# Pooled keys loaded on 128 partitions, and the steps of five blocks in one list

## The chip, the cores and the metric

The kernel runs on one NeuronCore of a Trainium2 chip. The metric is the device time of one execution in microseconds, as the median of several runs. A profile of one execution shows what each engine did: TensorE (PE) multiplies matrices into PSUM and loads weights (PEld), VectorE (DVE) and ScalarE (ACT) work on PSUM and SBUF, GpSimd (POOL) works on SBUF and issues the input loads, SyncE (SP) issues the stores and the transposes that a DMA makes.

## The reference

```python
# attention with keys and values averaged over groups of 8 positions
B, H, S, D = 8, 8, 576, 64;  Sp = S // 8          # 72 pooled positions
k_p = k.reshape(B, H, Sp, 8, D).mean(axis=3)
v_p = v.reshape(B, H, Sp, 8, D).mean(axis=3)
scores = q @ k_p.transpose(0, 1, 3, 2) / sqrt(D)
attn = softmax(scores)                            # over the 72 pooled positions
x = (attn @ v_p).transpose(0, 2, 1, 3).reshape(B * S, H * D)      # 4608 x 512
# feed-forward: the largest of three linear maps, then a fourth
h = maximum(maximum(x @ w1, x @ w2), x @ w3)      # w1, w2, w3: 512 x 768
out = h @ w_out                                   # 768 x 512, result 4608 x 512, float32
```

## The kernel before

The eight batches go through attention one by one, and their 576 tokens each fill a ring `xT` of 2048 columns (features on partitions, tokens along the free dimension). The feed-forward reads that ring in nine blocks of 512 tokens, numbered 0 to 8. Attention of batch n+1 is interleaved with the feed-forward of block n, so that PE always has matmuls to do while other engines finish exponentials, evictions and loads. Each engine executes its own instructions strictly in the order in which the program issues them; the order in the code is the order on the engine. Nothing reorders them: the order was written out by hand as lists of short names, and a small interpreter (`middle` for blocks 1 to 5, `weave` for the rest) turns each name into instructions.

What the names stand for, for a batch b (written `b:` where it isn't the block's own) or a block n:

- `k`: keys of the batch. `k-` turns the pooled keys `kp` with matmuls into PSUM (`keys`, `pkt`), `k+` copies them into the two padded tiles `kz` (`turn_k`, L213; DVE writes the first tile, ACT the second, for batches above 2).
- `T`: a DMA transpose, issued by SP, of the batch's queries `qb` into `qT` (L349). `q0` to `q3` do the same on PE, for batch 2.
- `s0`, `s3`, `s6` (and `s70` to `s78` for batch 7): scores on PE (L226), and with `+` their exponentials on ACT (L231) into `et`.
- `v0` to `v4`: the attention output of one 128-token chunk on PE (`values`, L302), with `+` its normalization on DVE (L310, L312) into `xn`.
- `x0` to `x4`: `xn` transposed into the ring `xT`; from batch 3 on by a DMA transpose from SP (L287).
- `h`: one piece of the hidden layer of a block: four matmuls of 512 columns (L419) and, with `+`, an ACT or DVE operation on the result (L425, L427).
- digits `1` to `7`: the seven products of a Strassen-like form of the output matmul (`out_seven`, L765), ten matmuls each, with their evictions to `osb` (L776, L779); `a1` to `a4` and `b1` to `b4` are the DVE sums these products need (`sums_of`, L664). In `weave`, `o1` to `o7` are the same for blocks 5 and 7, `1a` to `7c` are the seven products of the hidden layer (`seven`, L842), `T` there folds x for them, and `F` is one step of a plain projection (`project`, L467, L471).
- `f` and `S`: sums of weights on DVE that the seven-product forms need.
- `k5<`, `v5<`, `q5<`: the load of keys, values or queries of a batch, issued by POOL. Such a load waits for the last hidden matmul issued before it and for the latest query transpose `T`, and everything behind it on POOL waits with it.
- `k5+2`, `v5+2`: the next two operations of the pooling fold on POOL. `!` makes the next such operation wait for the last DVE sum (`gate`).

A name with `-` starts a step (its matmuls), the same name with `+` later ends it (the eviction); a name with neither does both.

POOL computes the pooled keys and values. A load brings keys of one batch as float16 into a tile [96, 6, 8, 64]: 96 partitions, six groups of eight positions each. `fold_steps` (L163 to L167) adds the eight rows of a group in three stages, 4+4 into `half`, 2+2, 1+1, for keys and values alike, the first stage in two operations for batches 3 to 7. Three PE transposes of [96, 128] then turn `kp`. Queries and keys use two buffers each, and so do `qT`, `kz`, `kp` and the tiles of values.

The list of before had one entry per block, 1 to 5; all hidden pieces, products and attention steps of a block's entry came before those of the next.

Of the kernel before, what the change touches and what calls it, by code (L numbers as in the profile page):

```python
# [10 lines left out]
ALU = mybir.AluOpType  # L11
# [3 lines left out]
def kernel(  # L15
# [11 lines left out]
    nc = tc.nc  # L27
# [4 lines left out]
    POOL = 8  # L32
# [40 lines left out]
    def load_k(b, eng, dtype=F16, parts=1):  # L73
# [5 lines left out]
        return [eng.dma_start(out=kts[b][:, i:i + n], in_=src[:, i:i + n])  # L79
                for i in range(0, 6, n)][-1]  # L80

    def load_v(b, eng, dtype=F16, cuts=(0, H)):
        if b == 0:
            vts[0] = ld.tile([96, 4096], dtype, name="vt0", tag="vt")[:, 0:3072].rearrange(
                "p (h i d) -> p h i d", h=H, i=6)
            src = v[0].rearrange("h (p i) d -> p h i d", i=6)
            return [eng.dma_start(out=vts[0][:, h:g], in_=src[:, h:g])
                    for h, g in zip(cuts, cuts[1:])][-1]
        vts[b] = ld.tile([Sp, H, POOL, D], dtype, name="vt", tag="vt")
        src = v[b].rearrange("h (sp j) d -> sp h j d", j=POOL)  # L90
        return [eng.dma_start(out=vts[b][:, h:g], in_=src[:, h:g])
                for h, g in zip(cuts, cuts[1:])][-1]
# [24 lines left out]
    make_identity(nc, ident)  # L117
    identh = const.tile([128, 128], F16, name="identh", tag="identh")
    make_identity(nc, identh)
    load_v(0, nc.gpsimd, cuts=(0, 4, 8))  # L120
    pick = const.tile([96, 6, 128], F16, name="pick", tag="pick")
    nc.gpsimd.memset(pick, 1.0)
# [9 lines left out]
    load_q(1)  # L132
    load_v(1, nc.gpsimd)
    load_q(2)
    load_k(2, nc.gpsimd)
    load_v(2, nc.gpsimd)


# [18 lines left out]
    def fold_steps(e, t, out, dtype=F32, parts=1):  # L157
        part, n = t.shape[:2]
        f = const.tile([part, n, 4, D], dtype, name="half" if dtype == F32 else "halfh",
                       tag="half" if dtype == F32 else "k16")  # L160
        for i in range(0, n, n // parts):
            at = slice(i, i + n // parts)
            yield e.tensor_tensor(out=f[:, at], in0=t[:, at, 0:4, :], in1=t[:, at, 4:8, :],  # L163
                                  op=ALU.add)
        yield e.tensor_tensor(out=f[:, :, 0:2, :], in0=f[:, :, 0:2, :],  # L165
                              in1=f[:, :, 2:4, :], op=ALU.add)
        yield e.tensor_tensor(out=out, in0=f[:, :, 0, :], in1=f[:, :, 1, :], op=ALU.add)  # L167

    def new_kp(b):
        kps[b] = sb2.tile([96, 6, D], BF16, name="kp", tag="kp")  # L170
# [34 lines left out]
        return pkt  # L205

    def turn_k(b):
        pkt = keys(b, ATT if len(pools) < 3 else SC)

        def put():  # L210
            for par, evac in enumerate((nc.vector.tensor_copy, nc.scalar.copy)):
                for odd in range(2):
                    (evac if b > 2 else nc.vector.tensor_copy)(  # L213
                        out=kz_all[b % 2][par][64 * par:64 * par + 64, :, 0:Sp].rearrange(
                             "p h (r i t) -> p h r i t", i=3, t=2)[:, :, :, :, odd],
                        in_=pkt[64 * odd:64 * odd + 64].rearrange(
                             "p i (h r) -> p h r i", r=12))

        return put
# [586 lines left out]
    def seven(n):  # L806
# [41 lines left out]
        def evict(i, g, p):  # L848
# [11 lines left out]
            elif i in (5, 7) and (12 - i, g) in done:  # L860
# [6 lines left out]
              15: [(0, "S S")], 17: [(1, "K")], 18: [(0, "S S")], 24: [(1, "q0 k")], 25: [(1, "q1")],  # L867
              26: [(1, "s0 q2")], 28: [(1, "s3 Q3")], 30: [(1, "s6")], 31: [(1, "v0")],
              32: [(1, "v1 x0")], 33: [(1, "X1 v2 v3")]}, (hidden, project))
    load_k(3, nc.gpsimd)  # L870
    load_v(3, nc.gpsimd)
    load_q(3)
    fold_k(2, nc.gpsimd)
    fold_v(2)


    folding = {}

    def pool_step(n, name):

        what, b = name[0], int(name[1])
        if name[2:] == "<":
            load = {"k": lambda: load_k(b, nc.gpsimd), "v": lambda: load_v(b, nc.gpsimd),
                    "q": lambda: load_q(b)}[what]
            op = load()
            for x in (mms[-1], *turned):
                after([op], x)
            return
        if (what, b) not in folding:
            if what == "k":  # L890
                new_kp(b)
                folding[what, b] = fold_steps(nc.gpsimd, kts[b], kps[b], parts=2)
            else:
                folding[what, b] = fold_steps(nc.gpsimd, vts[b], vp_all[:, b, :, 0:D],
                                                  parts=2)
# [4 lines left out]
            held.clear()  # L900

    ORDER = """
        b1 o1- 2a- b3 o1+ k7- b2 1a- 1b- v62- 1a+ k7+ 2a+ b4 T o6- s70- o6+ o2- s70+ o2+ 6a-
        s71- o5- 7a- s72- 7a+ vpool s71+ 6a+ 1b+ s72+ v62+ s73- v63- 5a- v63+ s74- 6b- x62
        s73+ s75- s74+ 5a+ v64 s76- s75+ x63 s76+ s77- 4a- s77+ s78- 3a- 4a+ 6b+ s78+ 2c-
        o7- o5+ 2b- o7+ x64 3a+ 1c- 5b- v70- o3- v70+ 1c+ x70 6c- 2b+ 6c+ 5b+ v71- o4- 2c+
        3b- o3+ o4+ 2a- T 7b- v71+ 7b+ x71 5c- 3b+ 2b- 5c+ v72- 4b- 1a 4b+ 3c- 7c- 2a+ 7c+
        v72+ 3c+ F 1b- 4c 1b+ v73 x72 6a- 2b+ 6b- 6a+ F 7a- 5a- F 5a+ 6b+ v74- 3a- v74+ x73
        7a+ 3a+ x74 F 1c- 4a- 1c+ 4a+ 2c- 5b 6c- 7b- 6c+ 7b+ 3b- T F 3b+ 2c+ 5c- 1a- 5c+ 4b
        1a+ F 7c 2a- 3c- 2c- 2a+ 3c+ 4c- 6a 4c+ 1b- H 2b- 5a- h 1b+ 5a+ 6b- 7a 3a 6b+ o1 1c-  # L910
        5b- 4a- 5b+ o2- 1c+ 6c- 4a+ 6c+ 7b- 2b+ 7b+ 3b- o6- 2c+ 5c- o6+ o2+ 4b- 5c+ o5- 4b+
        o5+ 7c o7- 3b+ 3c- 4c- o7+ o3- 4c+ o4- 3c+ o3+ o4+
    """

    def weave():

        products, seen, outs = {}, {}, out_seven(5)
        for name in ORDER.split():
            if name == "F":
                next(tiles)  # L920
            elif name == "vpool":
                held[:] = gate
                pool_step(5, "v7+4")
            elif name[0] == "b":
                sums_of(5, name)
            elif name == "H":
# [19 lines left out]
                else:  # L946
                    parts(name, begin)

    MIDDLE = {
        1: """  # L950
            h- q4< k4< h+ 1:x2 1:v4- h- h- v4< h+ 1:v4+ h+ h- 1:x3 h- h+ h+ h- 1:x4 h+ h- k-
            h- h+ h+ q0 h h- k+ h+ h q1 h s0- s0+ s0+ q2 h- s0+ h- s0+ h+ b1 S q3 h+ h- S S
            3:T S h+ a3 s3- a1 s3+ s3+ h- s3+ h- h+ h+ a2 h- s3+ a4 s6- s6+ 1- s6+ h+ b3 b2
            b4 v0 2- 1+ 6- x0 v1 7- v2- 6+ x1 5- 2+ 7+ v2+ ! k3+4 v3- v3+2 v3+ 5+ v4 3- x2
            4- x3 3+ 4+ x4
        """,
        2: """
            h k5< k- h- k+ h+ a1 a3 h- a2 f a4 f ! v3+2 v5< h+ f s0- s0+ s0+ s0+ h- h- h- h+
            h+ s0+ h- h+ s3- h+ h- f s3+ h- s3+ h+ h- s3+ b1 s3+ s6- h+ s6+ h- h+ h- s6+ !
            k4+2 h+ h+ b2 b3 b4 ! k4+2 1- 4:T v0- 1+ v1- v0+ x0 2- v1+ 6- v2- 7- x1 2+ 7+  # L960
            v4+2 6+ v2+ 5- v3- 5+ v3+ x2 x3 v4 x4 3- 4 3+
        """,
        3: """
            k- q5< k+ a3 k6< h a1 h- h- h+ a2 s0- f a4 ! v4+2 s0+ s0+ f h- h+ s0+ h+ s0+ h-
            h- h+ h+ s3- h- v6< h+ h s3+ s3+ s3+ s3+ h- b1 h- h+ h+ s6- s6+ ! k5+2 h h- s6+
            1- h+ b2 b3 b4 1+ ! k5+2 v5+2 v0- 2- v0+ x0 v1 6- 2+ x1 6+ 7- 5:T 7+ v2- 5- v2+
            x2 v3- 5+ v3+ v4 x3 3 x4 4
        """,
        4: """
            h- q6< h+ k- h- k+ a1 a2 f h+ h- a3 a4 ! v5+2 h- f h+ k7< h+ s0- s0+ h- h- s0+  # L970
            s0+ h+ s0+ h+ 6:T h- s3- h+ s3+ s3+ s3+ h- s3+ h+ h- b1 h+ h ! k6+2 s6- s6+ h h
            b3 b2 b4 s6+ ! k6+2 1- v6+2 v0 2- 1+ x0 v1- 6- v1+ 2+ x1 v2 7- 6+ 5- x2 v3 6:k-
            x3 7+ 5+ 3- 6:k+ v4 x4 4- 3+ 4+
        """,
        5: """
            h q7< a1 v7< h- a2 h- a3 h+ h+ a4 ! v6+2 h- s0- s0+ h+ s0+ h- s0+ s0+ h- h- k7+4
            h+ h+ s3- h+ 7:T s3+ h- s3+ h- s3+ s3+ h+ s6- h+ s6+ s6+ h h- v0 h+ h- x0 v1- h+
            v1+ x1
        """}
    folds = iter([f for wi in range(1, 3) for f in [fold_w(wi)] * 4])  # L980

    def middle(n):

        pieces, outs, out_tiles = hidden(n), None, project(n)
        for name in MIDDLE[n].split():
            if name[0] == "h":
                parts(name, lambda: next(pieces))
            elif name == "F":
                next(out_tiles)
            elif name == "f":  # L990
                next(next(folds))
            elif name == "!":
                held[:] = gate
            elif name[0].isdigit() and name[1:] in ("", "+", "-"):
                outs = outs or out_seven(n)
                parts(f"o{name}", lambda: outs(int(name[0]), 0, 1))
            elif name[0] in "ab":
                sums_of(n, name)
            elif name[2:3] == "<" or name[2:3] == "+" and name[3:]:
                pool_step(n, name)  # L1000
            else:
                b, _, step = name.rpartition(":")
                do(int(b or n + 1), step)
        assert next(pieces, None) is None

    tt_all.append(const.tile([128, 4, 5, HALF], F16, name="tt", tag="tt"))
    for n in range(1, 6):
        middle(n)
    assert next(folds, None) is None
    pad2 = const.tile([128, 3, 2, HALF], F16, name="pad2", tag="k16")  # L1010
    pad3 = ld.tile([128, 8, 2, HALF], F16, name="pad3", tag="vt")
# [47 lines left out]
```

## Time and profile before

| | us |
|---|---|
| median of 3 runs (226.77 to 227.67) | 226.8 |
| the profiled execution | 227.08 |
| its span, from the first to the last instruction | 225.4 |
| PE busy in the span | 212.3 |
| PE's last matmul ends | 221.5 |
| POOL busy in the span | 140.9 |

The TensorE clock was granted in full (1.0) through the whole span. In the 40 slices of the span, POOL's and PE's busy tenths read:

```profile
PE   6688999999999999999999999999799999999993
...
POOL 7974300999939969775885769794292903881020
PEclk9999999999999999999999999999999999999999
DMA  6999999999649999649967999699530755200265
```

PE is near its limit in all slices but the first four, the 29th and the last. The DMA engines are full until about 55 us while the weights and the first three batches arrive.

### The profile page before, as it was taken

The page shows a single profiled execution, that of the slowest core. Times are in us where ns is not written, and L with a number is a line of the kernel's source. Part 1 is how long each engine was busy: PE and PEld are TensorE (multiplying, and loading weights), DVE is VectorE, ACT ScalarE, POOL GpSimd, SP SyncE. Part 2 cuts the span into 40 slices and gives each one's busy share as a digit, 9 for nine tenths or more (in the row PEclk, how much of TensorE's full clock was granted, in tenths as well). Part 3 has the DMA queues.
Part 4 walks back from the last instruction along what each step waited for, and adds up shares of the span by engine and source line. Part 5 has one row for each costly group of instructions (what it writes and reads, how often), then busy time and mean ns, then how long its engine had stood idle before and what let it go on. Part 6 is the DMA issues. An engine that isn't in the chain of part 4 may idle for free.

```text
span 225.4 us, 4876 instructions
## 1 busy us (share of the span) xinstructions
PE 212.3 (94%) x1884; PEld 147.1 (65%) x1885; DVE 161.4 (72%) x314; ACT 120.3 (53%) x233; POOL 140.9 (63%) x121
## 2 busy tenths in 40 slices
PE   6688999999999999999999999999799999999993
PEld 2477744458658645964685468547589667788882
DVE  3668898036997796776679668729767977878940
ACT  2267524855883576237724842693694445564330
POOL 7974300999939969775885769794292903881020
PEclk9999999999999999999999999999999999999999
DMA  6999999999649999649967999699530755200265
GB/s 179 209 197 197 211 203 209 202 168 230 115 105 156 168 176 247 122 61 214 252 85 154 221 202 151 86 236 166 109 56 19 163 102 113 47 0 3 66 198 159
DMA packets 47303, 33.55 MB, mean 149 GB/s; under 512 B 26992, under 2 KB 42288, under 8 KB 47280
## 3 DMA queue, kind: packets, MB, share of 16 engines
q0 software_dynamic: 16944, 16.98, 47.8%
q1 hardware_dynamic: 29888, 15.87, 31.1%
q10 hardware_dynamic: 448, 0.39, 0.7%
q8 instruction: 15, 0.25, 0.5%
q14 instruction: 8, 0.07, 0.1%
HBM read 34.60 MB, written 9.44 MB: 195 GB/s over the span
## 4 chain that ended last, share of the span: by engine, by line
PE 58%; DMA 17%; DVE 10%; POOL 7%; ACT 3%; issue 3%; ACTq 0%; POOLq 0%; DVEq 0%
PE pw L419 17%; PE oA L765 12%; DMA vt<-in_v_dram 8%; PE oC L765 6%; PE pA L842 5%; DMA mw<-in_moe_w_dram 4%; DMA qT<-qb 4%; PE oB L765 3%; PE pC L842 3%; PE pav L302 2%; PE po L471 2%; PE psc L226 2%; POOL half L163 2%; DVE kz L213 2%; DVE tt L664 1%
## 5 line engine op out<-in xcount | busy, mean ns | idle before, releaser
L419 PE MATMUL pw<-xT,mw 128*128 128x512 f16 (+1 forms) x336 | 68.5, 349 | 0.3 <-ACT xT L296 0.2
L419 PEld LDWEIGHTS <-mw 128*128 128x128 f16 x336 | 30.7, 98 | 26.1 <-issue 1.8
L163 POOL TENSOR_TENSOR half<-vt 72x1024 f32<-72x1024 f16 (+1 forms) x12 | 29.1, 2444 | 20.8 <-DMA vt<-in_v_dram 13.3
L427 DVE TENSOR_TENSOR hT<-t,pw 128x512 f16<-128x512 f16 (+1 forms) x42 | 25.3, 608 | 19.1 <-PE pw L419 11.3
L231 ACT ACTIVATE et<-psc 72x512 f16<-72x512 f32 (+2 forms) x66 | 33.9, 571 | 6.7 <-PE psc L226 6.5
L165 POOL TENSOR_TENSOR half<-half 72x1024 f32<-72x1024 f32 (+1 forms) x13 | 28.1, 2165 | 12.6 <-DVE tt L664 5.2
L425 ACT ACTIVATE t<-pw 128x512 f16<-128x512 f32 (+1 forms) x42 | 22.6, 538 | 15.1 <-PE pw L419 14.5
L312 DVE TENSOR_TENSOR xn<-pav,rcp 128x512 f16<-128x512 f32 x40 | 27.6, 691 | 1.4
L776 ACT COPY osb<-oA 128x512 f32<-128x512 f32 x20 | 11.7, 587 | 20.1 <-PE oA L765 19.9
L851 ACT CAST pad<-pA 128x512 f16<-128x512 f32 x27 | 15.1, 585 | 11.7 <-PE pA L842 9.1
L765 PEld LDWEIGHTS <-tt 128*128 128x128 f16 x200 | 18.8, 98 | 2.1
L163 POOL TENSOR_TENSOR half<-ktFalse 96x768 f32<-96x768 f16 (+1 forms) x11 | 19.3, 1773 | 0.6 <-issue 0.5
L226 PEld LDWEIGHTS <-kz 64*128 64x128 bf16 (+1 forms) x161 | 8.9, 95 | 12.4 <-issue 7.2
L302 PEld LDWEIGHTS <-et 72*128 72x128 f16 x320 | 14.9, 98 | 3.0 <-issue 1.1
L302 PE MATMUL pav<-vp,et 72*128 72x65 f16 x320 | 16.3, 194 | 0.6 <-POOL vp L167 0.3
L310 DVE RECIPROCAL rcp<-pav 128x8 f32<-128x8 f32 x40 | 8.1, 201 | 11.3 <-PE pav L302 11.2
L842 PEld LDWEIGHTS <-sw 128*128 128x128 f16 x144 | 13.8, 98 | 2.7 <-issue 0.2
L822 DVE SCALAR_TENSOR_TENSOR hT<-pad 128x512 f16<-128x512 f16 x18 | 14.0, 785 | 1.1 <-ACT pad L855 0.5
L819 DVE TENSOR_TENSOR pad<-pad,pC 128x512 f16<-128x512 f16 x18 | 12.3, 681 | 3.5 <-PE pC L842 2.7
L226 PE MATMUL psc<-qT,kz 64*128 64x256 bf16 (+5 forms) x138 | 13.3, 263 | 1.0 <-DVE qT L197 0.9
L616 POOL TENSOR_TENSOR pad<-xT 128x256 f16<-128x256 f16 x8 | 5.5, 687 | 13.1 <-DMA xT<-xn 13.1
L765 PEld LDWEIGHTS <-hT 128*128 128x128 f16 x126 | 12.3, 98 | 1.4
(122 smaller groups left out, 400.6 us busy)
## 6 DMA issues: line engine op xcount, KB each, us to landing
out_dram<-osb SPq DMA_DIRECT2D x32, 128.0 KB, 4.6
ktFalse<-in_k_dram POOLq DMA_DIRECT2D x7, 576.0 KB, 9.1
qb<-in_q_dram POOLq DMA_DIRECT2D x7, 576.0 KB, 7.6
vt<-in_v_dram POOLq DMA_DIRECT2D x7, 576.0 KB, 11.8
out_dram<-osb SPq DMA_DIRECT2D x11, 256.0 KB, 6.8
mw<-in_moe_w_dram POOLq DMA_DIRECT2D x9, 256.0 KB, 9.2
ktTrue<-in_k_dram SPq DMA_DIRECT2D x3, 384.0 KB, 5.1
out_dram<-ob SPq DMA_DIRECT2D x8, 128.0 KB, 2.9
```

The source lines that it names most:

```text
L163: yield e.tensor_tensor(out=f[:, at], in0=t[:, at, 0:4, :], in1=t[:, at, 4:8, :], op=ALU.add)
L165: yield e.tensor_tensor(out=f[:, :, 0:2, :], in0=f[:, :, 0:2, :], in1=f[:, :, 2:4, :], op=ALU.add)
L226: nc.tensor.matmul(out, kz_all[b % 2][f % 2][rows, h, :], qTs[b][rows, n + i0:n + i1, 64 * (h % 2):64 * (h % 2) + 64], start=True, stop=True)
L231: nc.scalar.activation(out=out, in_=in_, func=FT.Exp, scale=1.0 / 64.0)
L302: nc.tensor.matmul(pav[:, h // 4, 65 * (h % 4):65 * (h % 4) + 65], ets[b][:, h, c0:c0 + 128], vp_all[:, b, h, :], start=True, stop=True)
L312: nc.vector.tensor_tensor(out=xn, in0=pv[:, :, :, 0:D], in1=rcp.to_broadcast([128, 2, 4, D]), op=ALU.mult)
L419: mm = nc.tensor.matmul(pw, w_sb[wi][:, kc, bass.ts(jc, 128)], x[:, kc], start=(kc == 0), stop=(kc == KCH - 1))
L425: yield lambda t=t, pw=pw: nc.scalar.activation(out=t, in_=pw, func=FT.Relu)
L427: yield lambda t=t, pw=pw: nc.vector.tensor_tensor(out=hT[:, jc, c0:c1], in0=t, in1=pw, op=ALU.max)
L765: nc.tensor.matmul(p, left, right, stop=(r == 4), skip_group_check=True, start=(i in FIRST and r == 0 and (m == 0 or n == LAST)))
L842: mm = nc.tensor.matmul(p[:, w], a[:, kc, bass.ts(g, 128)], b[:, kc, :], start=(i in FIRST and w + kc == 0), stop=(w + kc == 2), skip_grou ...
L851: nc.scalar.copy(out=kept(i, g), in_=p)
```

## The change

Two things change together.

Keys of batches 2 to 7 are loaded into a tile [128, 9, 4, 64]: each group of eight positions is cut in two halves of four, and the two halves lie 64 partitions apart. A partition then holds nine half groups. `fold_four` on POOL adds the four rows of a half in two stages. The matmuls that turn the keys use the tile `both` (two identity matrices of 64, one above the other) in place of an identity matrix, so that the sum over 128 partitions adds the two halves of each group: five matmuls with 64 columns in place of three transposes with 96, into float32 PSUM in place of bfloat16. The copies into `kz` follow the new layout.

The entries of blocks 1 to 5 become one list, in which a step names its block (`3/h-`) and its batch (`4:v0-`), and its order is new throughout, across the former limits of the blocks too. The list `ORDER` for the last part is new as well. The steps are the same ones; the folds of keys have three operations in place of four.

```diff
+    def load_k4(b, eng):
+        kts[b] = ld.tile([128, 9, POOL // 2, D], F16, name="kt4", tag="ktFalse")
+        src = k[b].rearrange("h s d -> (h s d)").rearrange(
+            "(c r e j d) -> e c r j d", c=64, r=9, e=2, j=POOL // 2)
+        return eng.dma_start(out=kts[b], in_=src)
...
+    both = const.tile([128, 64], F16, name="both", tag="both")
+    nc.gpsimd.tensor_tensor(out=both, in0=identh[:, 0:64], in1=identh[:, 64:128], op=ALU.add)
     load_v(0, nc.gpsimd, cuts=(0, 4, 8))
...
+    def fold_four(e, t, out):
+        n = t.shape[1]
+        f = const.tile([128, 9, 2, D], F32, name="half4", tag="half")
+        for a, z in ((0, 5), (5, 9)):
+            yield e.tensor_tensor(out=f[:, a:z], in0=t[:, a:z, 0:2, :],
+                                  in1=t[:, a:z, 2:4, :], op=ALU.add)
+        yield e.tensor_tensor(out=out, in0=f[:, :, 0, :], in1=f[:, :, 1, :], op=ALU.add)
+
+    def new_kp4(b):
+        kps[b] = sb2.tile([128, 9, D], F16, name="kp4", tag="kp4")
+
+    def keys4(b, tag):
+        pkt = psum([128, 5, 64], F32, name="pkt", tag=tag[0], bufs=tag[1])
+        for i in range(5):
+            n = min(2, 9 - 2 * i)
+            nc.tensor.matmul(pkt[0:64 * n, i, :],
+                             kps[b][:, 2 * i:2 * i + n, :].rearrange("p i d -> p (i d)"),
+                             both, start=True, stop=True)
+        return pkt
...
     def turn_k(b):
-        pkt = keys(b, ATT if len(pools) < 3 else SC)
+        pkt = (keys if b < 2 else keys4)(b, ATT if len(pools) < 3 else SC)
...
+                    if b > 1:
+                        (evac if b > 2 else nc.vector.tensor_copy)(
+                            out=kz_all[b % 2][par][64 * par:64 * par + 64, :, 0:Sp].rearrange(
+                                "p h (c r) -> p h c r", r=9)[:, :, :, odd:9:2],
+                            in_=pkt[64 * odd:64 * odd + 64, 0:5 - odd].rearrange(
+                                "p i (h c) -> p h c i", c=8))
+                        continue
...
     ORDER = """
-        b1 o1- 2a- b3 o1+ k7- b2 1a- 1b- v62- 1a+ k7+ 2a+ b4 T o6- s70- o6+ o2- s70+ o2+ 6a-
-        s71- o5- 7a- s72- 7a+ vpool s71+ 6a+ 1b+ s72+ v62+ s73- v63- 5a- v63+ s74- 6b- x62
-        s73+ s75- s74+ 5a+ v64 s76- s75+ x63 s76+ s77- 4a- s77+ s78- 3a- 4a+ 6b+ s78+ 2c-
-        o7- o5+ 2b- o7+ x64 3a+ 1c- 5b- v70- o3- v70+ 1c+ x70 6c- 2b+ 6c+ 5b+ v71- o4- 2c+
+        1a- k7- b1 o1- v62- 2a- 1b- o1+ 1a+ b3 b2 k7+ b4 o6- 1b+ 2a+ o6+ s70- T s70+ o2- 6a
+        s71 o5- v62+ o2+ s72- 7a- v63- s73- s72+ 5a- v63+ 7a+ s73+ x62 s74- 5a+ 6b- s75- s74+
+        v64- s75+ s76- 3a- 4a- 6b+ s76+ v64+ o5+ vpool 5b- 4a+ s77- s78- x63 5b+ o7- x64 s77+
+        s78+ 2c- o7+ 2b- 3a+ 1c v70- o3- 3b- v70+ 2b+ 6c- v71- 2c+ v71+ x70 6c+ 3b+ x71 o4-
...
-    MIDDLE = {
-        1: """
-            h- q4< k4< h+ 1:x2 1:v4- h- h- v4< h+ 1:v4+ h+ h- 1:x3 h- h+ h+ h- 1:x4 h+ h- k-
...
-        5: """
-            h q7< a1 v7< h- a2 h- a3 h+ h+ a4 ! v6+2 h- s0- s0+ h+ s0+ h- s0+ s0+ h- h- k7+4
-            h+ h+ s3- h+ 7:T s3+ h- s3+ h- s3+ s3+ h+ s6- h+ s6+ s6+ h h- v0 h+ h- x0 v1- h+
-            v1+ x1
+    MIDDLE = """
+        3:T k4< 1/h 1/h 1:x2 1:v4- 1/h 1/h- 1:x3 1/h+ 2:k- 1/h- 1:v4+ q4< 1/h+ v4< 1/h 1/h
...
+        5:s0+ 4/h+ 5:s3- 4/b1 5:s3+ 4/h- 4/h- 5:s3+ 5:s3+ ! k6+2 5:s3+ 4/h+ 4/a4 4/h- 4/h+
+        4/h+ 5:s6- 4/b3 5:s6+ 5:s6+ 4/b2 4/1 4/2- 5:v0- 4/b4 4/6- 5:v1- 5:v0+ 5:v1+ 5:v2- !
+        k6+1 4/6+ 5:v2+ 5:x0 v6+2 4/2+ 4/5- 4/7- q7< 4/5+ 5:x1 5:v3- 6:k- 5:x2 4/7+ 4/3 5:v3+
+        4/4- 5:v4- 6:k+ 5/a1 5/h- 5/h- 5/h+ 4/4+ 5:v4+ 6:s0- 5/a3 ! v6+2 5/a2 6:s0+ k7+2 k7+1
+        5/h+ 5/a4 5/h- v7< 6:s0+ 6:s0+ 5/h- 6:s0+ 5:x3 5/h+ 5:x4 5/h+ 6:s3- 6:s3+ 6:s3+ 5/h-
+        6:s3+ 5/h- 6:s3+ 7:T 5/h+ 5/h+ 5/h- 6:s6- 6:s6+ 5/h- 5/h- 5/h+ 5/h+ 6:s6+ 6:v0- 6:v1-
+        5/h- 6:v0+ 5/h- 6:v1+ 5/h+ 5/h- 5/h+ 5/h+ 6:x0 6:x1 5/h+
     """
```

## The prediction

> **What bounds the kernel now.** I read the busy shares first, then the list of waits on PE, then the chain of waits, then the queues around its widest hole.
>
> ```profile
> PE 212.3 (94%) x1884; PEld 147.1 (65%) x1885; DVE 161.4 (72%) x314; ACT 120.3 (53%) x233; POOL 140.9 (63%) x121
> ```
>
> PE is busy for 212.3 of 225.4 us, and POOL, whose work the change cuts, only for 140.9. So a faster POOL pays only where PE waits for something late. The waits on PE (total us, times, longest):
>
> ```profile
> PE psf L226 <- DMA qT<-qb: 1.6, 1, 1.6
> ...
> PE pxt L293 <- DVE xn L312: 1.2, 4, 0.4
> ...
> PE oA L765 <- ACT osb L776: 0.7, 4, 0.3
> PE psf L226 <- ACT et L231: 0.5, 1, 0.5
> PE pC L842 <- DVE pad L819: 0.4, 1, 0.4
> ...
> PE pav L302 <- DVE xn L312: 0.2, 1, 0.2
> ```
>
> These six lines hold 4.6 us, 4.0 of it behind the first 30 us. That is nearly all that an order can win: most of the rest of PE's idle time lies before 30 us or after its last matmul (221.5). The 1.6 us is the first score of batch 7 waiting for its turned queries. POOL's timeline shows what was asked for ahead of it:
>
> ```profile
> 142.89 0.79 POOL L99 DMA_DIRECT2D qb<-in_q_dram  x1 [0.96 <-PE pw L419]
> 144.11 0.85 POOL L91 DMA_DIRECT2D vt<-in_v_dram  x1 [0.44 <-issue]
> 144.98 2.36 POOL L165 TENSOR_TENSOR half<-half 72x1024 f32<-72x1024 f32 x1
> 147.42 1.27 POOL L167 TENSOR_TENSOR vp<-half 72x512 f16<-72x512 f32 x1
> 148.77 3.23 POOL L163 TENSOR_TENSOR half<-ktFalse 96x768 f32<-96x768 f16 x2
> 152.07 1.81 POOL L165 TENSOR_TENSOR half<-half 96x768 f32<-96x768 f32 x1
> 153.96 0.99 POOL L167 TENSOR_TENSOR kp<-half 96x384 bf16<-96x384 f32 x1
> 162.01 4.20 POOL L163 TENSOR_TENSOR half<-vt 72x1024 f32<-72x1024 f16 x2 [7.06 <-DVE pad L616]
> 166.29 2.35 POOL L165 TENSOR_TENSOR half<-half 72x1024 f32<-72x1024 f32 x1
> 168.71 1.60 POOL L167 TENSOR_TENSOR vp<-half 72x512 f16<-72x512 f32 x1
> ```
>
> The chain of waits, ACT's timeline and PE's timeline (start, us, what) show what came of it:
>
> ```profile
> 150.51 9.21 DMA qT<-qb
> ```
>
> ```profile
> 158.05 0.96 ACT L213 COPY kz<-pkt 64x288 bf16<-64x288 bf16 x2 [0.98 <-DVE kz L213]
> ```
>
> ```profile
> 159.85 0.38 PE L226 MATMUL psf<-qT,kz 128*128 128x320 bf16 x2 [1.60 <-DMA qT<-qb]
> ```
>
> Queries 7 are asked for at 142.89 and take 7.6 us to land; their turning starts at 150.51 and takes 9.2 us, because the load of values 7, asked for at 144.11 and 13.6 us on its way, runs beside it. The same turning took 4.0 us for batch 3 and 5.1 for batch 5. Two things stand just behind it: the keys of batch 7 are not copied before 159.01, and the fold of values 7 ends at 170.31, 0.4 us before PE multiplies with them (first chunk at 170.76).
>
> **The change part by part.** To place a moved step I laid both lists out in PE work, by the chain's pieces: 0.86 us for four 512-column matmuls, 1.09 for an output product, 0.26 for values, 0.5 to 0.6 for scores. The old list runs from 51.2 us at 1.04 times this work; the new list holds the same work, so a step's place gives a time at this pace.
>
> *Keys, on POOL.* Now 3.23+1.81+0.99 = 6.0 us a batch. New: halves of 640 and 512 elements and one add of 576. At 1.64/768 and 0.99/384 us an element this is 1.38+1.14+1.42 = 3.95 us, 2.1 less a batch. The load's issue grows: 0.54 us for 96 rows, 0.78 for 512 pieces (q), 0.86 for 576 (v); on that line 1152 pieces cost 1.2 to 1.3, and 0.54 is the lower end. Its landing is bounded by 6.0 (the quickest k) and twice v's 7.2. Both are covered: the new loads go out 11 to 25 us before their folds, and the folds end 2 to 5 us before PE turns the keys, with one exception. Keys 2 are turned after 2.4 us of the list instead of 3.9: due at 53.2, while POOL (free at 46.9, three loads in 2.8, fold 3.95) ends at 53.7. Cost 0.5, from 0 to 1.0. Against it, one more hidden piece stands ahead of the first turn of the block, where PE waited 0.24 for xn (at 51.67): -0.2.
>
> *Keys, on PE.* Three transposes become five matmuls of 64 columns, six times. Neither the shape nor the sum in PSUM is in the trace. The nearest row is eight values matmuls of 65 columns, each with its own weights, in 0.26 us: 33 ns each; the three transposes take 0.13. 5x33-130 = 35 ns a batch, 0.2 us in all, from 0 to 2.1 (should each 98 ns weight load show: 6x(0.49-0.13)). The page "TensorE: Matmul & The Clock Gate", section "Back-to-back issue gap", of the Trainium skill says that a stream of weight load and matmul sustains about 81 ns at 128 columns, which speaks against this change; by it the estimate would be 6x(0.41-0.13), 1.6 us. The row of 33 ns says otherwise, and I take the row.
>
> *Copies to kz.* 320 and 256 elements in place of 288 twice, from f32 in place of bf16; the f32 copies at L509 take 0.48 like the bf16 ones. Nothing. *The tile `both`.* One 64-column add on POOL ahead of the first loads; the nearest row is 0.67 us for 256 columns, so about 0.2. It is covered while the DMA queue stays full to 48 us, but the chain runs through these issues: 0.1, from 0 to 0.2.
>
> *Queries and values 7.* The new list asks for q7 earlier (after 83.7 us of work, not 87.4), but on POOL behind the turning of batch 6 and the first half of fold v6. That puts it at about 141, landing at 149, as before or 1.5 us better. The load of v7 moves behind the rest of v6 and the fold of k7: the gate after `5/a3` opens at about 144.7, then 3.6 for v6, 3.95 for k7, so 152.3 instead of 144.1. The turning now has the engines almost to itself: 4 to 5 us, ready at 154, 4 us before it is needed. The next late thing is kz of batch 7. `k7-` is 1.1 us of PE work earlier, but on DVE it still stands behind `b1 b3 b2`; these start at about 155.0 since the norms of batch 6 now come before the last hidden piece, so DVE copies until 157.4 and ACT until 158.4, against PE's 158.3. Of 1.6 us I count 1.5, from 0.6 (kz at 159.0 again) to 1.6.
>
> The price: v7 lands 7.2 us after 152.3 at best (as v6's did), its fold takes 8.3 (162.01 to 170.31), ending at 167.8. PE comes to `v70` 10.9 us after the first score of batch 7, 10.4 without the et wait, so at 168.8. At v's median of 11.0 the fold ends at 171.6, 2.8 late; at 13.6 it is 5.4 late. Little else is loading then, so I take +0.5, from 0 to 5.4. By the fit in the page "DMA: Bandwidth & Descriptors", section "Anatomy of one DMA", of the Trainium skill (2.0 us and bytes over 436e3) the 1.18 MB would land in an estimated 4.7 us and this term be 0. No v load here was quicker than 7.2.
>
> *The rest of the order.* The score waiting for et: one 0.59 us eviction of a product leaves ACT's queue between the scores (`1b+` now stands ahead of `s70`): -0.5, from -0.5 to 0. The waits for pad and xn around 178 to 181: two projections stand earlier as cover, while DVE's work and POOL's `pad` beside it stay: -0.3 of 0.6, from -0.6 to +0.5. The waits for osb: blocks 2 to 4 now have another product between 5 and 3, but blocks 3 and 4 have only two values steps between 6 and 5: -0.2, from -0.7 to +0.3. Queries 5 and 6 are ready 1 to 5 us ahead, the turned x of blocks 4 and 5 within 1 us of need: +0.3, from 0 to 1.0.
>
> One thing more: POOL has 8 us less to do (6x2.1 less 6x0.7 of issue), and DVE's adds of two SBUF inputs wait less for it: such an add of 512 elements took 2.58 us beside a fold (59.69) and 0.41 alone (63.61). -0.5, from -1.5 to 0.
>
> Sum: -1.5 +0.5 (v70) +0.5 -0.2 (keys 2) +0.2 +0.1 -0.5 -0.3 -0.2 +0.3 -0.5 = -1.6: the profiled span goes from 225.4 to 223.8. That execution took 227.08 us, what lies around the span with it, and the median of the runs is 226.8; against the median the forecast is 225.2.
>
> **The rivals.** *A: the hole only narrows.* Keys 7 are again late on DVE (1.5 becomes 0.6), and et, pad and osb wait as before (1.0 lost). -1.6+0.9+1.0 = +0.3: 227.1. For it: DVE is at 80% from 160 to 180. Against: the products ahead of `s70` were moved. *B, slower: the hole moves to v70.* v7 is asked for 8 us later and PE needs it at a fixed place; if its load shares the engines with the turning and x transposes as it did before, it lands in 12.3 us (between 11.0 and 13.6), the fold ends at 172.9, 4.1 after need: -1.6-0.5+4.1 = +2.0, 228.8. It decides for slower from a landing of 11.5 us on. Against it: the turning should be over by 154. *C: every wait in the list goes* and v70 is in time: of the six lines 4.0 us, less 0.3 for the matmuls and `both` and 0.3 for keys 2: -3.4, 223.4. Against: PE's own products leave DVE no more slack there. *D: the weight loads show*, 2.1 us: -1.6+1.9 = +0.3, 227.1. The values rows speak against it, and as much against the 226.6 (-1.6+1.4) that the page's 81 ns would give.
>
> **How the numbers follow.** Forecast 0.47 (its own range 224.3 to 226.1), A 0.22, B 0.15, C 0.13, D 0.03. A measurement here can tell 0.5%, 1.1 us: faster is below 225.7, slower above 227.9. The forecast gives 0.40 to faster and 0.07 to same; C 0.13 faster; A 0.03 faster, 0.17 same, 0.02 slower; B 0.12 slower, 0.03 same; D same. Faster 0.56, same 0.30, slower 0.14. The range takes in A and most of C and the near part of B: 223.2 to 228.0.
>
> **What would show it.** Right: q7's turning lands in 4 to 6 us and before 156; PE has no wait for qT; kp adds of 1.4 us; five key matmuls in 0.17 us. Wrong: PE waits for vp at the first values of batch 7, or for kz at its first score; a k load that lands later than its fold is due; key matmuls near 100 ns.

## The result and the profile after

The changed kernel takes 347.2 us (median of 4 runs, 345.0 to 350.0) against 226.8 before: a ratio of 1.530, 95% interval 1.518 to 1.542. The profiled execution took 346.99 us, its span is 345.3. The forecast was 225.2, the range 223.2 to 228.0. For the runs further down, medians and ratios leave out executions that took over 1.5% longer than the fastest of their kernel; the expectations, written earlier, quote medians of all.

The first and second part of the page of the changed kernel (busy time, then the busy tenths of 40 slices of 8.6 us):

```profile
PE 236.2 (68%) x1897; PEld 156.4 (45%) x1897; DVE 165.4 (48%) x314; ACT 120.6 (35%) x233; POOL 152.1 (44%) x117
...
PE   7899992039950798246971900895295859999995
...
PEclk9999998559995599665996765698589689999999
```

PE was at 94% of its span before and is at 68% now. It stands still again and again, about once a batch, and in those slices its granted clock falls to half. That also makes the same work longer: 236.2 us busy in place of 212.3.

The waits on PE (total us, times, longest):

```profile
PE pkt L194 <- POOL kp L185: 58.8, 5, 20.8
PE pw L456 <- DMA xT<-xn: 18.3, 2, 10.9
PE psc L263 <- DMA qT<-qb: 18.0, 1, 18.0
PE pA L879 <- DVE pad L653: 3.5, 1, 3.5
```

PE waits five times for pooled keys. POOL makes them late because the keys land late; the view of the tile `kt` and the list of DMA issues (count, KB each, median us to landing) say how late:

```profile
L87 POOL DMA_DIRECT2D kt<-in_k_dram x6: 4440/4448/4492, 24.0 to 218.4; - x6
...
DMA to landing us min/median/max: 30.6/35.8/46.5
```

```profile
qb<-in_q_dram POOLq DMA_DIRECT2D x7, 576.0 KB, 22.5
vt<-in_v_dram POOLq DMA_DIRECT2D x7, 576.0 KB, 26.1
kt<-in_k_dram POOLq DMA_DIRECT2D x6, 576.0 KB, 35.8
```

Before, the issue of such a load took 0.54 us on POOL and the landing 9.1 us (median), with 7.6 for queries and 11.8 for values. Queries and values were loaded as before, but those issued behind a key load land with it: keys 3, asked for at 64.94, land at 95.94, values 3 at 96.23, queries 4 at 99.04.

What the load does meanwhile is seen in the DMA view of a stretch in which little else moves, from 88 to 95 us:

```profile
DMA packets 340, 0.17 MB, mean 25 GB/s; under 512 B 0, under 2 KB 340, under 8 KB 340
...
q0 software_dynamic: 340, 0.17, 18.2%
```

Pieces of 512 B, 49 of them in a microsecond, their time 18% of sixteen engines: 2.9 pieces in flight. The weight loads, cut in pieces of the same size, have about 23 in flight (from 14 to 22 us in the kernel before). So about an eighth of the engines, two, carry the load. The page's count of the same queue over the whole span bears on what the other fourteen do:

```profile
DMA packets 102023, 33.75 MB, mean 98 GB/s; under 512 B 75376, under 2 KB 97584, under 8 KB 102000
...
q0 software_dynamic: 71664, 17.18, 44.8%
```

Before, it was 16944 packets and 16.98 MB. The 0.20 MB more, and nearly all packets more, are tiny ones: the counts below come to 48384 packets of 4 B, which fits 6 loads x 14 engines x 576 pieces. The packets do not name their engine.

Why two: the source is read as `(c r e j d) -> e c r j d`. For one half `e` the pieces of all `c` and `r` lie 512 elements apart, so `c` and `r` are one dimension of 576, and the pattern is [2, 576, 256] with the half outermost. That the size 2 of this outermost dimension sets the number of engines is theory A of the experiments. It is also what the Trainium skill states, "DMA: Bandwidth & Descriptors", section "Why a DMA increments its semaphore by 16 and not by 1": the engines used are the largest number up to 16 that divides the slowest dimension of both sides. The runs agree with it, here with 31 to 47 us of landing. The prediction did not weigh this rule.

### The profile page after: what moved, and what is told of

Its sections match the earlier page's. It is cut to its first block, busy times and chain, and to the rows that moved or that the text cites. A ratio compares the mean times of both kernels' runs of the same rounds, so it can differ in the third digit from the quotient of the medians.

```text
span 345.3 us, 4888 instructions
## 1 busy us (share of the span) xinstructions
PE 236.2 (68%) x1897; PEld 156.4 (45%) x1897; DVE 165.4 (48%) x314; ACT 120.6 (35%) x233; POOL 152.1 (44%) x117
## 3 DMA queue, kind: packets, MB, share of 16 engines
q0 software_dynamic: 71664, 17.18, 44.8%
## 4 chain that ended last, share of the span: by engine, by line
DMA 43%; issue 21%; POOL 16%; PE 16%; DVE 2%; ACT 0%; POOLq 0%; DVEq 0%; SPq 0%
DMA kt<-in_k_dram 23%; DMA qb<-in_q_dram 8%; DMA vt<-in_v_dram 5%; POOL half L172 4%; DMA xT<-xn 3%; PE oA L802 3%; PE pA L879 3%; POOL half L183 3%; DMA mw<-in_moe_w_dram 3%; POOL half L174 2%; PE po L508 2%; PE pC L879 2%; PE oC L802 2%; DMA qT<-qb 1%; POOL pad L653 1%
## 5 line engine op out<-in xcount | busy, mean ns | idle before, releaser
L456 PE MATMUL pw<-xT,mw 128*128 128x512 f16 (+1 forms) x336 | 78.7, 387 | 18.5 <-DMA xT<-xn 18.3
L456 PEld LDWEIGHTS <-mw 128*128 128x128 f16 x336 | 33.6, 106 | 52.4 <-issue 32.3
L87 POOL DMA_DIRECT2D kt<-in_k_dram x6 | 26.7, 4458 | 65.2 <-DMA kt<-in_k_dram 25.9
L194 PE MATMUL pkt<-both,kp 128*128 128x64 f16 (+1 forms) x30 | 3.4, 236 | 58.8 <-POOL kp L185 58.8
L194 PEld LDWEIGHTS <-kp 128*128 128x128 f16 (+1 forms) x30 | 2.1, 118 | 60.4 <-POOL kp L185 59.9
L183 POOL TENSOR_TENSOR half<-kt 128x640 f32<-128x640 f16 (+1 forms) x12 | 15.5, 1318 | 21.2 <-DMA kt<-in_k_dram 21.1
L244 DVE CAST kz<-pkt 64x320 bf16<-64x320 f32 (+1 forms) x14 | 6.8, 485 | 37.3 <-PE pkt L194 37.2
L106 POOL DMA_DIRECT2D qb<-in_q_dram x9 | 7.1, 792 | 35.3 <-DMA qT<-qb 33.0
L802 PEld LDWEIGHTS <-tt 128*128 128x128 f16 x200 | 20.3, 105 | 4.3 <-issue 0.5
L813 ACT COPY osb<-oA 128x512 f32<-128x512 f32 x20 | 11.8, 588 | 25.2 <-PE oA L802 25.0
L174 POOL TENSOR_TENSOR half<-half 72x1024 f32<-72x1024 f32 x7 | 16.7, 2380 | 7.5 <-DVE tt L701 7.2
L888 ACT CAST pad<-pA 128x512 f16<-128x512 f32 x27 | 15.7, 589 | 11.4 <-PE pA L879 5.8
```

The lines of the kernel that those rows point to most:

```text
L87: return eng.dma_start(out=kts[b], in_=src)
L183: yield e.tensor_tensor(out=f[:, a:z], in0=t[:, a:z, 0:2, :], in1=t[:, a:z, 2:4, :], op=ALU.add)
L456: mm = nc.tensor.matmul(pw, w_sb[wi][:, kc, bass.ts(jc, 128)], x[:, kc], start=(kc == 0), stop=(kc == KCH - 1))
L802: nc.tensor.matmul(p, left, right, stop=(r == 4), skip_group_check=True, start=(i in FIRST and r == 0 and (m == 0 or n == LAST)))
```

## The experiments

The kernel of before, run beside them, took 227.1, 227.4 and 227.4 us on the three chips used.

**e1_halves: the same bytes into the same tile, in two transfers.**

```diff
-        return eng.dma_start(out=kts[b], in_=src)
+        return [eng.dma_start(out=kts[b][64 * e:64 * e + 64], in_=src[e])
+                for e in range(2)][0]
```

> The changed kernel, with each key load of batches 2 to 7 issued as two loads of 64 partitions (one for each half of the groups) in place of one load whose outermost source dimension is 2. Pieces (1152 of 512 B), folds and order stay. Theory A (the load ran on 2 of the 16 DMA engines): a pair lands 7 to 10 us after its issue instead of 31 to 46, PE no longer waits for kp or qT, and the time is 224 to 227 us. Theory B (the many small pieces, or their descriptors made by POOL, are slow wherever they go): landings stay near 30 us and the time above 320. Theory C (the new order issues loads too late): landings fall, but the time stays above 240.

230.5 us, ratio 1.0145 (1.0106 to 1.0184); a second set of runs of the same kernel (e1b_halves) gave 231.1 us, 1.0177 (1.0131 to 1.0223).

> The same kernel as e1 once more, for a second profile: a ratio of 1.010 to 1.018 to the kernel before, and again PE waiting for the first folded x of block 6 (2.1 us, x transposes of batch 6 landing 7 to 8 us after their issue beside the load of values 7), for hT beside a fold of keys (1.3) and for the x of block 4 (0.7).

The waits came again in its profile, with 1.8, 1.3 and 0.5 us.

The tile `kt` in the profile of e1_halves, and its queue:

```profile
L87 POOL DMA_DIRECT2D kt<-in_k_dram x12: 727/748/787, 23.5 to 129.7; - x12
...
DMA to landing us min/median/max: 4.6/6.6/20.8
```

```profile
q0 software_dynamic: 23376, 16.98, 51.3%
```

The 20.8 is the first load, among the weights. The extra packets are gone: 71664 - 23376 and 96 for six transfers fewer (16 each) is 48384. So 116 of the 120 us were the load. But some 3 to 4 us over before remain, where I had expected 224 to 227.

**e5_two_by_two: two transfers again, but each with the half outermost.** If the number of transfers, their size or the issue in two were what mends e1_halves, this one would be mended too.

```diff
+            "(a c r e j d) -> a e c r j d", a=2, c=32, r=9, e=2, j=POOL // 2)
+        return [eng.dma_start(out=kts[b][64 * a:64 * a + 64], in_=src[a])
+                for a in range(2)][0]
```

> Like e1 two loads of 64 partitions a batch, the same 1152 pieces of 512 B, but each load brings both halves of 32 groups, so that its outermost source dimension is 2 again (the partitions are numbered anew, and the tile both follows). Theory A: each load uses 2 engines, the two together 4 if they fall on different ones: landing about half of 31 to 36 us, 15 to 20, and a time between 230 and 290; on the same two engines as slow as the changed kernel. Theory B: like e1, whatever e1 gives.

284.0 us, ratio 1.250 (1.246 to 1.255), within the 230 to 290 of theory A; the landing is longer than its 15 to 20. The tile `kt` and the queue of this kernel:

```profile
L87 POOL DMA_DIRECT2D kt<-in_k_dram x12: 2465/2484/2532, 23.8 to 170.9; - x12
...
DMA to landing us min/median/max: 18.1/25.7/30.9
```

```profile
q0 software_dynamic: 71760, 17.18, 61.5%
```

Transfers, their sizes and pieces are as in e1_halves; only the outermost dimension is 2 again. Each issue takes 2.48 us in place of 0.75, the landing 25.7 in place of 6.6, and 71760 - 23376 = 48384 = 12 x 14 x 288 tiny packets are back, which fits one for each piece of an engine that works, on each of fourteen that do not. Theory B, which expected this kernel to go like e1_halves, is out; theory A stands.

**e8_old_order_one_load: the slow load in the order of before.** It differs from e4_keys below only in the transfer.

> The order of before with the keys of batches 2 to 7 loaded as in the change, one transfer of 1152 pieces a batch (the kernel e4_keys, 227.7 us, has two transfers of 64 partitions and differs in nothing else). Theory A (a transfer that 2 of the 16 engines carry lands after 31 to 47 us, and later loads of the queue with it; the order has little to do with it): the landing of the key loads is again 30 us or more, POOL's issue of one 4.4 us, PE waits for kp for more than 40 us in all, and the time lies above 300 us. Theory H (the slow load costs so much only because the new order asks for keys late or puts other loads behind them): with the old order most of the landing is hidden and the time lies under 270 us.

348.0 us, ratio 1.531 (1.525 to 1.537). Its two longest waits on PE:

```profile
PE pkt L194 <- POOL kp L185: 45.8, 4, 20.3
PE pav L339 <- POOL vp L176: 33.0, 3, 22.1
```

The 120 us do not come from the new order: the old one loses as much, partly at the values, which are queued behind the keys.

**e4_keys: the new keys (loaded as in e1_halves) in the old order; e3_order: the new order with the old keys.** Together with e1_halves they part the two halves of the change.

> The old order with the new keys, loaded as in e1. Theory A: between 225.5 and 227.5 us, since POOL was not what PE waited for and the five matmuls cost 0.03 us a batch; the wait for the turned queries of batch 7 (1.6 us) stays. Theory B: above 300 us. Theory C: like A.

> The new order with the old keys (96 partitions, three transposes; each fold in three operations of 3.1, 1.8 and 1.0 us). Theory A: no slow load, so 224 to 230 us; the old fold is 2 us longer, so key steps of batches 2, 3 and 5 may come late by up to 2 us each. Theory B: the same. Theory C: above 240 us.

e4_keys: 227.5 us, ratio 1.0024 (0.9993 to 1.0054), no measurable change. e3_order: 241.4 us, 1.062 (1.059 to 1.065). The main waits on PE in e3_order:

```profile
PE pxt L330 <- DVE xn L349: 4.0, 4, 3.1
PE pw L456 <- DVE hT L464: 2.3, 1, 2.3
PE pkt L232 <- POOL kp L176: 1.7, 1, 1.7
PE oA L802 <- DVE tt L701: 1.7, 2, 1.2
```

The new order needs the shorter folds: with the old ones it loses 14 us, where I had expected 224 to 230 us. Keys 2 are late on POOL by the 1.7. The longest wait, 3.1, is one for DVE beside POOL: three DVE sums take 7.0 us (68.02 to 75.05) beside the fold of keys 3 (68.18 to 74.63), and 1.5 in e1_halves (68.16 to 69.66), where that fold begins at 72.39. With the new folds the new order is still about 3 us slower than the old order with the same keys.

In e4_keys POOL is busy 6.3 us less, and yet nothing is gained. Part of the answer is on PE itself. The turning of one batch's keys and what follows it, in PE's timeline of before and then of e4_keys (start, us, what):

```profile
77.28 0.29 PE L202 MATMUL pkt<-ident,kp 96*128 96x96 bf16 x3
77.41 1.89 PE L419 MATMUL pw<-xT,mw 128*128 128x512 f16 x8
```

```profile
77.83 0.43 PE L195 MATMUL pkt<-both,kp 128*128 128x64 f16 x5
78.19 1.90 PE L457 MATMUL pw<-xT,mw 128*128 128x512 f16 x8
```

From the first of them to the matmul behind them it was 0.13 us and is 0.36: 0.23 more a batch, 1.4 in six, about what the whole order was meant to win. (In e4_keys it is 1.1: the turning of keys 6 is followed by a wait for ACT that was there before.) The 0.36 is not spread evenly. By the starts in the trace the first four matmuls come 29 ns apart (77.834, 77.863, 77.892, 77.921), the pace of the values matmuls. The fifth turns the ninth half group alone, with weights of 64 columns in place of 128:

```profile
78.04 0.22 PE L195 MATMUL pkt<-both,kp 128*64 128x64 f16 x1
```

It starts 123 ns behind the fourth, and the next one 149 ns behind it. All six batches of e10_k5_late show the same. So three quarters of the 0.36 lie around one narrow matmul. That the width of its weights is the reason was not tried. The other part is that the old hole is still there. The first score of batch 7 in e4_keys:

```profile
160.25 0.38 PE L264 MATMUL psf<-qT,kz 128*128 128x320 bf16 x2 [0.75 <-DVE tt L702]
```

The sum that the line names ends at 160.24, but it did not release the score: the weight load ahead of the score, which waits for DVE too, had begun at 160.22. What came last is the turned queries: the turning begins at 151.49 and lands at 160.12, as late as before (150.51 and 159.71), with values 7 and four stores beside it as before; the score starts 0.13 us behind the landing in both. PE arrives later, having done more work by then, and waits 0.75 us in place of 1.60. The score starts at 160.25 against 159.85: most of the matmuls' price is paid out of this hole, and a faster POOL has nothing to shorten.

**Where the new order loses.** The waits on PE in e1_halves:

```profile
PE pA L880 <- DVE pad L654: 2.1, 1, 2.1
PE wm L527 <- DVE warm L123: 1.5, 1, 1.5
PE pw L457 <- DVE hT L465: 1.3, 1, 1.3
PE pav L340 <- POOL vp L177: 1.3, 1, 1.3
...
PE pw L457 <- DMA xT<-xn: 0.7, 1, 0.7
PE pA L880 <- POOL pad L654: 0.7, 1, 0.7
PE pkt L195 <- POOL kp L186: 0.6, 1, 0.6
```

The waits for the queries of batch 7, for `et` and for `pC` (2.5 us before) are gone, but new ones have come. Behind the first 30 us PE waits 7.4 us here and 4.0 before. I tried the three largest of these.

*e6_both_late*: the tile `both` is made behind POOL's first loads, in case its add delays them and so values 1 (the 1.3 at `pav`).

> e1 with the tile both made behind the first loads of POOL instead of ahead of them. Theory D (the extra POOL operation delays the first loads and with them the values of batch 1, for which PE waits): 0.3 to 1.0 us faster than e1, and PE's wait for vp at 47 us back from 1.3 to 0.3. Theory E (those loads are queued anyway, the later landing was chance): no change against e1.

1.0141 (1.0096 to 1.0187); the wait is 1.1 us. Nothing shown beyond the scatter. The tile is not the reason: e3_order makes it ahead of the loads too, and there values 1 land at 39.07 us, as before (39.00). In the profiles with the new key loads they land between 39.5 and 41.1; why was not tried.

*e7_v7_first*: the load of values 7 just ahead of that of queries 7, in case it is what makes the x transposes of batch 6 late (the 2.1 at `pA`).

```diff
-        v6+2 4/2+ 4/5- 4/7- q7< 4/5+
+        v6+2 4/2+ 4/5- 4/7- v7< q7< 4/5+
...
-        5/h+ 5/a4 5/h- v7< 6:s0+
+        5/h+ 5/a4 5/h- 6:s0+
```

> e1 with the load of values 7 issued just ahead of the queries 7 instead of behind the fold of keys 7. Theory F (the load of values 7 beside the turning of queries 7 and the x transposes of batch 6 makes PE wait for the folded x): values 7 land before 154, queries 7 about 153, their turning takes 4 to 5 us, the x transposes 2.4 us each, the wait of 2.1 us for the folded x goes, 1.5 to 2.5 us faster than e1. Rival G (DVE or another transfer holds the x transposes): they stay at 7 us and the time at e1's.

The first two x transposes of batch 6 did fall from 8.3 and 7.4 us to 2.4 each, and the turning of queries 7 from 6.9 to 4.6. But the last two of batch 5 (issued at 148.61 and 150.21) now ran beside both loads. They landed at 160.58 and 160.85, behind queries 7 (160.08), after 12.0 and 10.7 us in place of 7.3 and 4.9, and PE waited for them instead:

```profile
PE pA L880 <- DMA xT<-xn: 2.0, 1, 2.0
```

232.1 us, 1.0204 (1.0159 to 1.0250): the hole moves, and nothing is gained.

*e10_k5_late*: the first part of the fold of keys 5 put behind the sum `3/a1`.

```diff
-        3:x0 ! k5+2 2/7+
+        3:x0 2/7+
...
-        4:s0+ 4:s0+ 3/a1 3/h-
+        4:s0+ 4:s0+ 3/a1 ! k5+2 3/h-
```

> e1_halves (the change with each key load as two transfers; 231.5 to 233.7 us) with one step moved: the first two operations of the fold of keys 5 stand behind the sum 3/a1 and wait for it, so POOL no longer adds while DVE makes that sum. Theory I (DVE's add of two SBUF inputs is held by POOL's adds: 2.81 us at 102.1 beside the fold at 103.2, and PE then waits 1.3 us for DVE's hidden piece): the sum takes 0.5 us or less, PE's wait for hT on its lines of 512 columns falls from 1.3 to under 0.4, and the time falls by about 1, to 230.5 to 232.7. Rival J (the sum is slow for a reason of its own, or the fold put later makes keys 5 or values 5 late): the wait stays above 1 us, or a new one of at least 1 us for kp or vp appears, and the time stays.

229.7 us, ratio 1.0110 (1.0077 to 1.0144). DVE's timeline around that sum, in e1_halves and then in e10_k5_late:

```profile
102.10 2.81 DVE L702 TENSOR_TENSOR tt<-xT 128x512 f16<-128x512 f16 x1
104.83 1.27 DVE L465 TENSOR_TENSOR hT<-t,pw 128x512 f16<-128x512 f16 x2
```

```profile
102.83 0.41 DVE L702 TENSOR_TENSOR tt<-xT 128x512 f16<-128x512 f16 x1
103.39 0.69 DVE L465 TENSOR_TENSOR hT<-t,pw 128x512 f16<-128x512 f16 x1 [0.15 <-PE pw L457]
```

The same sum takes 2.81 us beside POOL's fold and 0.41 with the fold moved away. It ends at 104.91, 0.29 us behind the fold's first add (103.21 to 104.61). Why it was not done in the 1.1 us ahead of that add stays open; POOL's issue of a load ran there, as it does beside the 0.41. The wait of 1.3 us for `hT`, which the profiles of e1_halves and e1b_halves both have, is gone. Theory I holds in this: the place of the fold made one short DVE add slow, and that cost PE 1.3 us. The gain in time is 0.8 to 1.4 us by the medians, but the intervals overlap, so it is not shown clear of the scatter. The wait of 2.0 us for `vp` in this profile is the one for values 1, at 48.75 us, which e1b_halves has with 2.1 too, and not rival J's.

**e9_keys_v7_late: e4_keys with the load of values 7 behind the fold of keys 7,** an attempt to beat both kernels.

```diff
-            h q7< a1 v7< h- a2
+            h q7< a1 h- a2
...
-            ... s0+ s0+ h- h- k7+4
+            ... s0+ s0+ h- h- k7+4 v7<
```

> e4_keys (the order of before, new keys by two transfers) with one step moved: v7< stands behind k7+4 instead of between a1 and h-, so that the load of values 7 goes out at about 153.7 us instead of 144.7. Theory of the prediction (values 7 beside the turning of queries 7 make the turning slow): the turning takes 4 to 6.5 us instead of 8.6, its end moves from 160.1 to 156 to 158, and values 7 land between 161 and 165, so that their fold, gated at 162.5, starts less than 3 us late. Gain bounded by the wait of 0.7 us in front of the first score of batch 7 that e4_keys has for another reason (a DVE sum), so 226.6 to 228.2 us, a ratio of 0.995 to 1.003 to before. Rival: the turning is slow because of the four stores beside it, takes over 8 us again, and values 7 are late at their fold by the full 7 to 9 us of their landing: 229 to 231 us.

229.6 us, ratio 1.0115 (1.0072 to 1.0159). The values went out at 154.95, 1.5 us behind the start of the turning of queries 7 (153.43), and the turning took 11.4 us in place of the 4 to 6.5 expected, longer than that of batch 7 in any other run. (The DVE sum of the expectation is the line of e4_keys that names the wrong releaser, as said above.) PE waited for the turning:

```profile
PE psf L264 <- DMA qT<-qb: 4.1, 1, 4.1
```

The time is in the rival's range, but its reason, the four stores, does not account for the 11.4 us: they had landed by 155.63, and the turning ended at 164.82, 0.3 us ahead of the values (165.12). Why the same turning, with the values 1.8 us behind its start, was over after 6.9 us in e1_halves is not shown. No version here beats the kernel of before.

## Why the prediction was wrong

**The step that failed: "Keys, on POOL", the load.** It put the issue at "1152 pieces cost 1.2 to 1.3" and said of the landing that it "is bounded by 6.0 (the quickest k) and twice v's 7.2. Both are covered". Measured: 4.45 us and 30.6 to 46.5. Both bounds came from loads whose outermost dimension is 72 or 96 partitions, and the cost was scaled by bytes and pieces. The pattern of the new load was never written out in the order in which the DMA walks it; its first dimension is 2, though the tile has 128 partitions. e1_halves, e5_two_by_two and e8_old_order_one_load show that this alone is 116 of the 120 us. With that bound the sum left a late key load no more than 1.0 us, and no rival held the case either, although "a k load that lands later than its fold is due" stood in the list of what would show it wrong.

With the load mended the rest can be read, and there too the forecast was too low: 225.2 against 229.7 to 231.1 us. Step by step:

- *Folds on POOL*: right. Predicted 1.38 + 1.14 + 1.42 us; 1.41, 1.16 and 1.40 in e4_keys. (The two rates named there give 1.37, 1.09 and 1.49; the sum is the same.)
- *Copies to kz*: right, 0.48 us.
- *Keys, on PE*: mis-sized, 0.2 us predicted, 1.4 measured. The 33 ns a matmul, taken from the rows of `pav`, hold for the four wide ones (29 ns). What the term left out is the fifth, whose weights are half as wide: 123 ns ahead of it and 149 behind. The rule that the prediction set beside its own (the Trainium skill, "TensorE: Matmul & The Clock Gate", section "Back-to-back issue gap", about 81 ns and 1.6 us) came near the total, but by luck: none of the gaps is 81 ns. So did rival D, at 0.49 us a batch against 0.36: the four wide weight loads do not show.
- *Keys 2*: right, 0.5 predicted, 0.6 measured. *The tile `both`*: its add takes 0.3 us in e4_keys, not 0.2; values 0 go out 0.4 later there (4.38 for 3.98), but land at the same time (11.80 for 11.85).
- *Queries and values 7*: the named wait goes (e1_halves has none), but the reason was half right. Alone, the turning takes 4.6 us (e7_v7_first, within the 4 to 5); the 10.2 and 10.0 us that it took for batches 4 and 6 before were left out. In the new order (e1_halves) queries 7 leave at 144.40, not 141, and values 7 at 155.64, not 152.3, so the turning, late as well, takes 6.9 us with the values beside it. The price was not paid at `v70`, as the +0.5 and rival B had it, but at a place I had not priced: "Little else is loading then" left out the x transposes of batch 6. Issued at 157.07 and 158.38 in e1_halves, with values 7 in flight until 165.20, they land at 165.34 and 165.75; in e4_keys, with the values home at 158.17, the first two take 2.5 and 2.4 us. This is the wait of 2.1 us for `pad`. Rival B had the sharing of load and transposes and the sign right, but not the place.
- *et, osb, x of blocks 4 and 5*: right. The wait for `et` is gone, `osb` falls from 0.7 to 0.5, and the ring costs 0.7 at one place (0.3, up to 1.0, was allowed). *pad and xn*: within the range; 0.6 before, 0.7 at another place in e1_halves, where 0.3 less was forecast. Of the six lines of waits 3.7 us lie behind the first 30 us; the 4.0 that rival C counts is that of all lines.
- *DVE beside POOL*: wrong in sign. I counted 0.5 gained, since POOL has less to do; the new order puts one fold beside one sum at the wrong moment and loses 1.3. An average over the span said nothing about the place.

What stays open: why values 1 land later with the new key loads, which gives the wait for `vp` (0.9 us in e4_keys, up to 2.1 in e1b_halves, 0.3 before). And the order of the change, mended, stays 2.5 to 4 us over before. The turning of keys (1.4), the slow sum (1.3) and the waits for `pad` (2.1) and for values 1 are what the traces offer against the 2.5 us of waits that are gone; that they add up to it is only argued from the lists.

## What to carry to other kernels

Write out the access pattern of a changed DMA as the engine walks it, merged dimensions and all, and look at its outermost size before scaling a landing time by bytes or pieces: 128 partitions on the SBUF side do not help when the other side begins with 2. A load that is slow in itself delays what is queued behind it, so check the landings of its neighbours first. And price a moved load against everything that is in flight at its new place, the small transposes too, not only against the transfer it was moved away from.

## What the runs showed of the hardware

- The slow load costs POOL, too: 4.45 us of issue in place of 2 x 0.75. It comes with 48384 packets of 4 B in six loads; their number fits one for each piece of a working engine on each of fourteen others. That these packets cost the issue was not tried.
- PE's clock. In the changed kernel PE stops at 99.5 us; the granted clock is 1.0 until 102.5 and 0.50 from 102.75. PE begins again at 114.44. The view of stretches (window, length, PE busy with its count, granted clock, DMA share, GB/s) shows that it works at half the clock until 119.8, for 5.4 us:

```profile
115.00:116.00 1.00, 1.00 (x4) 0.50 0.63 29
...
118.00:119.00 1.00, 1.00 (x7) 0.50 1.19 172
119.00:120.00 1.00, 1.00 (x4) 0.60 1.23 205
120.00:121.00 1.00, 1.00 (x6) 1.00 1.21 189
```

  Each long stop therefore costs a few microseconds beyond its own length. The wait of 4.1 us in e9_keys_v7_late does it as well (0.50 from 163.0 to 169.8), the 1.6 us of the kernel before does not. Length alone does not decide in between: the 2.1 us in e1_halves do it (0.50 from 167.2 to 170.6), the 2.0 us at 48.75 in e10_k5_late do not. The Trainium skill ("TensorE: Matmul & The Clock Gate", section "Part 1: The HAM clock gate (the "warmup" mystery)") puts the warm-up at half the clock at about 3.4 us; 5.4 us were seen here.
- DMA transposes of x issued while a 576 KB load is in flight landed just after it: 0.1 to 0.6 us behind values 7 in e1_halves and e10_k5_late, after 7.1 to 8.3 us in place of 2.4, and 0.5 to 0.8 us behind queries 7 in e7_v7_first.
